# A linear-attention and softplus-MLP kernel: raw weights in two half tiles, four K buffers, and the second pass's attention a step earlier and ahead of softplus

## The chip, the cores and the metric

The kernel runs on one NeuronCore of a Trainium2 chip. The metric is the device time of one execution in microseconds. Before the change it was 609.94 us, the median of three runs (608.14 to 610.45).

## The reference

The reference is a delta-rule attention followed by a two-layer MLP on its output.

```python
B, H, S, D = 4, 8, 768, 48
k_n = k / (norm(k) + 1e-06)
state = zeros(B, H, D, D)
for t in range(S):
    y[:, :, t] = q_t @ state
    v_old = k_t @ state
    state = state + beta_t * outer(k_t, v_t - v_old)
x = y laid out as (B * S, H * D)          # 3072 x 384
h = x @ w_in                              # 384 x 2048
g = maximum(h, 0) + log1p(exp(-abs(h)))   # softplus
out = g @ w_out                           # 2048 x 384
```

## The kernel before

The sequence is cut into 12 chunks of 64 tokens (`NS`, `C`). A chunk of all 4 batches and 8 heads gives 256 rows of x, and each chunk has one MLP **pass** (0 to 11) over the 2048 hidden units, in 8 **steps** of two weight tiles of 128 units. Step (s, g) is step g of pass s.

One step puts out, in this order: the matmuls of `hidden(s, g)` with its three ScalarE functions (abs, exp, ln), a share of background work on DVE (`pull`, up to a budget in estimated ns), `softplus` of the step (one DVE instruction in pass 0, three after it, since g is then kept as a high and a low part), the attention blocks planned for the step, the conversion of weights (pass 0 alone), the splits of weights planned in `SPLITS`, and the output matmuls of the step before (`output(*late)`), which need that step's softplus. The order of the code is the order on each engine: the schedule is manual, and every engine works through its own list in order.

The attention of a chunk runs beside the MLP of the chunk before. It is a chain of blocks, placed by `at(s, g, cost, ...)`: `gram` (products of K with itself, for two chunks at a time), `invert` (the solution of 32 small triangular systems on DVE, in the background), `finish` (its two transposes), `cross_a` and `cross_b` (which join the half blocks), `arrange`, `masked_keys` (K against the state and Q, mask), `corrected` (the corrected values u), `result` (`y_all`, which makes x of that pass and moves parts of it by DMA, then `state` and the load of the next Q). `drain` runs the background to its end.

Weights come as 8-byte words of which two pieces make one f32: per tile one transfer into `ST[f]`, in the slot named `w{f+1}`. ScalarE copies the top piece (`top_half`, L402), DVE puts both together in place (`convert`, L410), and pass 0 multiplies with that f32 tile (`HF[f]`). From pass 1 on each f32 is used as a high part and a rest: `split(f)` casts on ScalarE into the first half of slot `w{f}` (L427) and subtracts on DVE into the second (L428). Slot `w{f}` held `HF[f-1]`, so tile f can be cast when tile f-1 has been subtracted. Three K buffers serve the chunks, with a fourth cut out of the slot behind the last weight tile from chunk 6 on. All DMAs are issued on SP, in order.

Of the kernel before, what the change touches and what calls it, by code (L numbers as in the profile page):

```python
# [40 lines left out]
def deltanet_moe(ctx, tc, kT, qT, kI, vN, beta, wts, out):  # L41
# [71 lines left out]

    n_tmp, spare = HB * HB // 4, []

    def last_slot():
        if not spare:
            assert len(W) == NF
            spare.append(one.tile([P, NP * C + 2 * n_tmp], F32, name=f"w{NF}"))
        return spare[0]  # L120

# [58 lines left out]
    def invert(u):  # L180
# [28 lines left out]
        if u < N16:  # L209

            parts = one.tile([P, 2, NP, HB + QB], F32, name=f"x{u + 1}")
            for j in range(2):
# [5 lines left out]
        if u < 2:
            tmp = (one, two)[u].tile([P, 2 * n_tmp], F32, name=("x0", "gl")[u])
        else:  # L220
            tmp = last_slot()[:, NP * C:]
# [165 lines left out]


    def load_weights(f):
        ST[f] = one.tile([P, 4 * DM], I32, name=f"w{f + 1}")  # L390
        if f >= AHEAD:
            nc.vector.tensor_copy(ST[f][:, 0:1], ST[f - AHEAD][:, 0:1])
        nc.sync.dma_start(ST[f].bitcast(U16)[:, 0:8 * DM - 1], wts[f][:, 1:8 * DM])

    def top_half(f):

        t, h = [a.bitcast(dt).rearrange("p (n w) -> p n w", w=w)  # L400
                for a, dt, w in ((tops[f % 2], F16, 2), (ST[f], BF16, 4))]
        nc.scalar.copy(t[:, :, 1], h[:, :, 2])  # L402

    def convert(n=1):
        for _ in range(n):
# [3 lines left out]
            words = ST[f].rearrange("p (n w) -> p n w", w=2)
            nc.vector.scalar_tensor_tensor(ST[f][:, 0:2 * DM], words[:, :, 0], 13, tops[f % 2],  # L410
                                           op0=ALU.logical_shift_right, op1=ALU.bitwise_or)
            HF[f] = ST[f][:, 0:2 * DM].bitcast(F32)
# [95 lines left out]
    with tc.manual_schedule(engines={ET.PE, ET.DVE, ET.Activation, ET.Pool, ET.SP}):  # L508
# [96 lines left out]

        def masked_keys(s, *gs):
            for g in gs:
                keys(s, g)
# [160 lines left out]
```

## Time and profile before

| | us |
|---|---|
| median of the runs | 609.94 |
| the profiled execution | 611.22 |
| its span (first to last instruction) | 609.5 |
| matmul engine (PE) busy | 569.4 (93%) |
| DVE busy | 447.4 (73%) |
| ScalarE (ACT) busy | 355.1 (58%) |
| GpSimd (POOL) busy | 31.2 (5%) |

The page of the profile gives for each group of instructions the busy time, the mean of one in ns, and the idle time of its engine ahead of it with what ended it. In the chain that ended last PE has 69%, DVE 17% and ACT 8%; the output matmuls (L474) have 28% and the hidden matmuls (L446) 27% of the span. Of the 40 slices of the span PE is busy at eight tenths or more in all but the first three, the tenth (seven) and the last; the granted clock is at seven tenths in the fifth slice and at eight in two around 137 to 168 us.

### The profile page before, as it was taken

Reading aid. Unit: us, or ns where it says so; the run is one execution under the profiler, and the core shown is the slowest. Engines: PE = TensorE matmul, PEld = TensorE weight load, DVE = VectorE, ACT = ScalarE, POOL = GpSimd, SP = SyncE. Lnnn points to the kernel's source line nnn. Section 1 sums busy time; section 2 is a strip of 40 time slices with the busy share of each in tenths; the row PEclk is TensorE's granted clock in tenths of the full one; section 3 lists DMA queues with packets and bytes.
Section 4 is the critical chain, followed back from the end, with each engine's and each line's share of the span. In section 5 each row is a group of like instructions: output and inputs, shape, how many; then the busy total and the mean of one; then the engine's idle time right before and its main releaser. Section 6 shows DMA issues by size and latency. Waiting matters only on the chain.

```text
span 609.5 us, 19848 instructions
## 1 busy us (share of the span) xinstructions
PE 569.4 (93%) x8630; PEld 531.0 (87%) x8630; DVE 447.4 (73%) x987; ACT 355.1 (58%) x703; POOL 31.2 (5%) x55
## 2 busy tenths in 40 slices
PE   5568899997889999999999999999999999999996
PEld 4447676797779999999999999999999999999996
DVE  5978679756677998989888989798888345354443
ACT  4344666776654767655766646775646485554443
POOL 5210000001000001000000000000000000000000
PEclk9999799998899999999999999999999999999999
DMA  9913851301042030132211141300120300300000
GB/s 201 320 55 104 247 205 53 68 29 27 27 89 84 9 61 29 54 67 80 43 26 54 36 91 49 67 29 9 48 66 28 66 30 2 66 29 14 27 0 27
DMA packets 33015, 39.81 MB, mean 65 GB/s; under 512 B 22432, under 2 KB 25600, under 8 KB 32928
## 3 DMA queue, kind: packets, MB, share of 16 engines
q1 hardware_dynamic: 32928, 38.54, 24.0%
q8 instruction: 68, 1.11, 0.8%
q14 instruction: 19, 0.16, 0.1%
HBM read 31.55 MB, written 4.72 MB: 60 GB/s over the span
## 4 chain that ended last, share of the span: by engine, by line
PE 69%; DVE 17%; ACT 8%; DMA 2%; issue 2%; SPq 1%; ACTq 0%; DVEq 0%
PE po L474 28%; PE ph L446 27%; PE pa L366 3%; PE pa L305 3%; DVE Z L233 2%; PE pa L351 2%; PE pa L339 2%; DVE w L410 2%; PE pa L131 2%; DVE w L228 2%; ACT w L427 1%; DVE big L317 1%; ACT a L451 1%; DVE a L457 1%; DVE w L428 1%
## 5 line engine op out<-in xcount | busy, mean ns | idle before, releaser
L446 PE MATMUL ph<-x,w 128*128 128x256 f32 x1680 | 229.5, 290 | 4.0 <-DMA x<-x 3.1
L446 PEld LDWEIGHTS ph<-x,w 128*128 128x128 f32 x1680 | 219.6, 191 | 10.4 <-issue 2.6
L474 PE MATMUL po<-w,gh 128*128 128x384 f32 x768 | 171.8, 364 | 3.9 <-DVE gh L459 3.9
L450 ACT ACTIVATE a<-ph 128x512 f32<-128x512 f32 x96 | 57.4, 598 | 169.4 <-PE ph L446 169.3
L474 PEld LDWEIGHTS po<-w,gh 128*128 128x128 f32 x768 | 133.3, 192 | 16.9 <-DVE gh L459 4.7
L457 DVE SCALAR_TENSOR_TENSOR a<-ph,a 128x512 f32<-128x512 f32 x88 | 60.4, 686 | 94.8 <-ACT a L452 94.7
L474 PE MATMUL po<-w,gl 128*128 128x384 f32 x352 | 78.4, 339 | 0.0
L474 PEld LDWEIGHTS po<-w,gl 128*128 128x128 f32 x352 | 63.8, 192 | 0.1
L460 DVE TENSOR_TENSOR gl<-a,gh 128x512 fp32r<-128x512 f32 x88 | 61.0, 693 | 3.0
L451 ACT ACTIVATE a<-a 128x512 f32<-128x512 f32 x96 | 60.7, 632 | 3.1
L452 ACT ACTIVATE a<-a 128x512 f32<-128x512 f32 x96 | 60.7, 632 | 3.1
L233 DVE TENSOR_TENSOR Z<-Z,w 128x30 f32<-128x30 f32 (+14 forms) x120 | 39.9, 332 | 4.1
L459 DVE CAST gh<-a 128x512 fp32r<-128x512 f32 x88 | 40.1, 456 | 3.0
L228 DVE TENSOR_TENSOR w<-Z,ltq 128x30 f32<-128x30 f32 (+14 forms) x120 | 39.6, 330 | 3.2
L317 DVE TENSOR_TENSOR big<-pa,maskP 64x256 f32<-64x256 f32 x88 | 37.0, 420 | 1.2
L366 PE MATMUL pa<-big 128*64 128x64 f32 x768 | 28.2, 232 | 1.1 <-ACT big L343 0.9
L366 PEld LDWEIGHTS pa<-big 128*64 128x64 f32 x768 | 25.7, 145 | 3.7 <-ACT big L343 1.8
L428 DVE TENSOR_TENSOR w<-w,w 128x768 fp32r<-128x768 f32 x16 | 15.3, 957 | 16.2 <-ACT w L427 16.1
L402 ACT CAST ex<-w 128x768 f16<-128x768 bf16 x16 | 16.8, 1060 | 17.7 <-DVE w L410 14.9
L285 POOL MEMSET tt<- 32x512 f32 x24 | 13.4, 558 | 265.6 <-ACT tt L283 262.2
L131 PE MATMUL pa<-kt 48*64 48x64 f32 x640 | 16.5, 261 | 11.1 <-DMA kt<-kT 10.9
L131 PEld LDWEIGHTS pa<-kt 48*64 48x64 f32 x640 | 14.7, 172 | 13.1 <-issue 7.6
(96 smaller groups left out, 538.9 us busy)
## 6 DMA issues: line engine op xcount, KB each, us to landing
w<-wts SPq DMA_DIRECT2D x16, 767.8 KB, 6.7
big<-qT SPq DMA_DIRECT2D x24, 192.0 KB, 4.2
nv<-vN SPq DMA_DIRECT2D x12, 384.0 KB, 3.4
ki<-kI SPq DMA_DIRECT2D x24, 192.0 KB, 4.6
out<-ex SPq DMA_DIRECT2D x24, 192.0 KB, 2.0
kt<-kT SPq DMA_DIRECT2D x20, 192.0 KB, 3.4
x<-x SPq DMA_DIRECT2D x66, 32.0 KB, 1.9
w<-kT SPq DMA_DIRECT2D x4, 192.0 KB, 4.3
```

The lines of the kernel that those rows point to most:

```text
L131: nc.tensor.matmul(pas[e][tk[t], i, :], k, k, start=True, stop=True)
L228: nc.vector.tensor_tensor(o, Z[:, a + j + 1:a + n, a + j:a + j + 1].to_broadcast([P, r, j]), lq[:, a + j:a + j + 1, a:a + j].to_broadcast( ...
L233: nc.vector.tensor_tensor(z, z, o, op=ALU.add)
L317: nc.vector.tensor_tensor(be[tk[ab], ab, e, 4 * g:4 * g + 4, 0:C], pks[e][t, :, 0:C], maskP[t].unsqueeze(1).to_broadcast([C, 4, C]), op=AL ...
L366: nc.tensor.matmul(py[tk[ab], i, :], big[:, at + C:at + 2 * C], big[:, at:at + C], start=True, stop=True)
L446: nc.tensor.matmul(ph[:, f], weight(s, 2 * g + f, a, k * P, P), xr[b][k], start=(c == 0), stop=(c == len(terms) * NK - 1))
L450: nc.scalar.activation(a, ph, AF.Abs)
L451: nc.scalar.activation(a, a, AF.Exp, scale=-1.0)
L452: nc.scalar.activation(a, a, AF.Ln, bias=1.0)
L457: nc.vector.scalar_tensor_tensor(a, ph, 0.0, a, op0=ALU.max, op1=ALU.add)
L460: nc.vector.tensor_tensor(hi_lo[1], a, hi_lo[0], op=ALU.subtract)
L474: nc.tensor.matmul(PO[s][:, h, 0:DM], hi_lo[b][:, f, h * P:(h + 1) * P], weight(s, 2 * g + f, a, DM, DM), start=(g == 0 and f == 0 and i = ...
```

## The change

It has four parts.

1. Raw weights come in two transfers per tile, into two half tiles: `RA[f]` in slot `a{f+1}` and `RB[f]` in slot `b{f}`. The copy of the top pieces and the conversion are each done in two halves; the converted tile lies in `RA[f]`. The high part goes into slot `b{f}`, where raw words lay that are no longer needed, the low part into slot `a{f}`, which held the converted tile f-1. Casts and subtractions have lists of their own, `HIGHS` and `LOWS`.
2. Four K buffers throughout; chunk 3's K is loaded near the start, chunk 4's where chunk 3's was. The scratch of the inversion has a tile of its own, and x has two buffers instead of three.
3. In pass 1 the attention blocks of chunk 2 stand one step earlier; the Gram matmuls of chunk 4 move from (0,7) to (0,4), those of chunk 5 from (1,5) to (0,7), where the next inversion also enters the background.
4. Softplus stands behind the blocks of its step instead of ahead of them, in every pass, and so behind the emptying of the background in the first step of odd passes, which pass 1 now has in this form too.

```diff
-STEP, EARLY, PULL0 = 3100, (4400, 3500, 3500), (500, 500, 3000)
-SPLITS = ((), (0,), (1,), (), (), (2,), (3,), (4,), (5,), (6, 7, 8), (9, 10), (11, 12), (13, 14), (15,), (), ())
+STEP, EARLY, PULL0 = 3100, (4100, 3500, 3500), (500, 500, 3000)
+HIGHS = {3: (0,), 4: (1,), 5: (2,), 6: (3, 4), 7: (5, 6), 8: (7, 8), 9: (9, 10), 10: (11,), 11: (12,), 12: (13, 14), 13: (15,)}
+LOWS = {6: (0,), 7: (1, 2, 3), 8: (4, 5, 6), 9: (7, 8, 9), 10: (10,), 11: (11,), 12: (12, 13), 13: (14, 15)}
...
-        kts[s] = KT[s if s < 2 else (1, 2, 3 if s > 2 else 2, 0)[s % 4]]
+        kts[s] = KT[s % 4]
...
+    tmp = const.tile([P, 2 * n_tmp], F32, name="tmp")
...
-        x = X[s] = one.tile([P, NK, n, B, C], ty, name=f"x{s % 3}")
+        x = X[s] = one.tile([P, NK, n, B, C], ty, name=f"x{s % 2}")
...
-        ST[f] = one.tile([P, 4 * DM], I32, name=f"w{f + 1}")
+        RA[f] = one.tile([P, 2 * DM], I32, name=f"a{f + 1}")
+        RB[f] = one.tile([P, 2 * DM], I32, name=f"b{f}")
         if f >= AHEAD:
-            nc.vector.tensor_copy(ST[f][:, 0:1], ST[f - AHEAD][:, 0:1])
-        nc.sync.dma_start(ST[f].bitcast(U16)[:, 0:8 * DM - 1], wts[f][:, 1:8 * DM])
+            nc.vector.tensor_copy(RA[f][:, 0:1], RA[f - AHEAD][:, 0:1])
+        for i, t in enumerate((RA[f], RB[f])):
+            nc.sync.dma_start(t.bitcast(U16)[:, 0:4 * DM - 1],
+                              wts[f][:, 4 * DM * i + 1:4 * DM * (i + 1)])
...
-    def split(f):
-
-        w = W[f] = one.tile([P, 2, 2 * DM], F32R, name=f"w{f}")
-        nc.scalar.copy(w[:, 0], HF[f])
-        nc.vector.tensor_tensor(w[:, 1], HF[f], w[:, 0], op=ALU.subtract)
+    def high(f):
+        assert f < done[0]
+        W[f, 0] = one.tile([P, 2 * DM], F32R, name=f"b{f}")
+        nc.scalar.copy(W[f, 0], HF[f])
+
+    def low(f):
+        W[f, 1] = one.tile([P, 2 * DM], F32R, name=f"a{f}")
+        nc.vector.tensor_tensor(W[f, 1], HF[f], W[f, 0], op=ALU.subtract)
...
         load_ki(0)
+        load_k(3)
         load_weights(1)
...
-        at(0, 7, 0, bind(load_beta, 2), bind(systems, 2), bind(gram, 4))
-        at(1, 0, 0, drain)
-        at(1, 1, 0, bind(cross_a, 2), bind(cross_a, 3))
-        at(1, 2, 920, bind(cross_b, 2), bind(cross_b, 3), bind(scale_v, 3), bind(arrange, 2))
-        at(1, 3, 2400, bind(masked_keys, 2, 0), bind(arrange, 3))
-        at(1, 4, 2400, bind(masked_keys, 2, 1))
-        at(1, 5, 0, bind(corrected, 2))
-        at(1, 6, 1700, bind(result, 2), bind(load_k, 6))
-        at(1, 5, 0, bind(gram, 5), bind(start, 2, invert), pos=1)
+        at(0, 4, 0, bind(load_beta, 2), bind(systems, 2), bind(gram, 4))
+        at(0, 7, 0, bind(gram, 5), bind(start, 2, invert))
+        at(1, 0, 0, bind(cross_a, 2), bind(cross_a, 3))
+        at(1, 1, 920, bind(cross_b, 2), bind(cross_b, 3), bind(scale_v, 3), bind(arrange, 2))
+        at(1, 2, 2400, bind(masked_keys, 2, 0))
+        at(1, 3, 2400, bind(masked_keys, 2, 1), bind(arrange, 3))
+        at(1, 4, 0, bind(corrected, 2))
+        at(1, 5, 1700, bind(result, 2))
...
-                softplus(s, g)
-                if s > 2 and s % 2 and g == 0:
+                if s % 2 and g == 0:
...
                 for block in blocks[0]:
                     block()
+                softplus(s, g)
...
-                for f in splits:
-                    split(f)
+                for f in highs:
+                    high(f)
+                for f in lows:
+                    low(f)
```

SP's list at the start, where the loads of K (kt), of weights (w), of V, Q and of K in its other layout (ki) are issued. Before:

```order
L100 DMA ki<-kI 64x768 x2
L393 DMA w_106<-wts 128x3071
L393 DMA w_219<-wts 128x3071
L88 DMA kt_74<-kT 48x1024 x2
L104 DMA nv<-vN 128x768
```

And now:

```order
L98 DMA ki<-kI 64x768 x2
L86 DMA kt_77<-kT 48x1024 x2
L386 DMA a_112<-wts 128x1535
L386 DMA b_113<-wts 128x1535
L386 DMA a_229<-wts 128x1535
L386 DMA b_230<-wts 128x1535
L102 DMA nv<-vN 128x768
```

The load of chunk 3's K has moved ahead of the second and the sixth weight tile, into a buffer of its own, and each weight tile has two transfers.

ScalarE's list in pass 1, from the functions of step (1,1) to those of step (1,3); casts of weights write w before, b now. Before:

```order
L450 ACTIVATE a<-ph 128x512
L451 ACTIVATE a<-a 128x512
L452 ACTIVATE a<-a 128x512
L277 ACTIVATE off<-pa 32x8x32 x8
L427 CAST w_1676<-w_603 128x768
L427 CAST w_1679<-w_691 128x768
L427 CAST w_1682<-w_799 128x768
L450 ACTIVATE a<-ph 128x512
L451 ACTIVATE a<-a 128x512
L452 ACTIVATE a<-a 128x512
```

And now:

```order
L452 ACTIVATE a<-a 128x512
L285 COPY tt<-pa 32x8x32 x8
L272 COPY tt<-tt 32x16x32 x2
L424 CAST b_1878<-a_941 128x768
L424 CAST b_1880<-a_1042 128x768
L450 ACTIVATE a<-ph 128x512
L451 ACTIVATE a<-a 128x512
L452 ACTIVATE a<-a 128x512
L424 CAST b_1953<-a_1049 128x768
L450 ACTIVATE a<-ph 128x512
```

Before, step (1,1) has the copies of cross_a and three casts; now it has those of cross_b, the copies of arrange and two casts, and step (1,2) has one.

DVE's list around step (3,5), which makes x of chunk 4 (x is the rest that is subtracted; the softplus of the step writes a, gh and gl). Before:

```order
L457 SCALAR_TENSOR_TENSOR a<-ph,a 128x512
L459 CAST gh<-a 128x512
L460 TENSOR_TENSOR gl<-a,gh 128x512
L374 TENSOR_TENSOR x_3470<-pa,x_3470 128x3x128
L376 TENSOR_TENSOR x_3471<-pa,x_3471 128x128
L374 TENSOR_TENSOR x_3470<-pa,x_3470 128x3x128
L376 TENSOR_TENSOR x_3471<-pa,x_3471 128x128
L228 TENSOR_TENSOR w_2217<-Z,ltq 128x108
```

And now:

```order
L222 TENSOR_TENSOR Z<-Z,tmp 128x4x27
L363 TENSOR_TENSOR x_3546<-pa,x_3546 128x3x128
L365 TENSOR_TENSOR x_3547<-pa,x_3547 128x128
L363 TENSOR_TENSOR x_3546<-pa,x_3546 128x3x128
L365 TENSOR_TENSOR x_3547<-pa,x_3547 128x128
L457 SCALAR_TENSOR_TENSOR a<-ph,a 128x512
L459 CAST gh<-a 128x512
L460 TENSOR_TENSOR gl<-a,gh 128x512
L217 TENSOR_TENSOR tmp<-Z,ltq 128x130
```

The four subtractions for x now stand ahead of the step's softplus, and the background (L217 and L222, before L228 and L233) follows.

## Rows read from the trace of the kernel before

**Rows 1.** Windows: passes 0, 1, 2, 4 and 5, from their first hidden matmul to the next pass's, and two microseconds in pass 1. Columns: length, then busy time of PE, PE's weight loads, DVE, ACT and POOL (with numbers of instructions), granted clock of PE as a share, share of the DMA engines, GB/s.

```profile
56.50:117.50 61.00, 56.39 (x731) 41.01 (x729) 48.00 (x103) 38.95 (x68) 1.03 (x2) 0.92 0.45 137
117.50:174.60 57.10, 50.47 (x815) 46.46 (x813) 34.12 (x54) 42.15 (x83) 3.45 (x5) 0.94 0.14 37
174.60:223.70 49.10, 46.17 (x625) 44.10 (x625) 42.65 (x109) 26.31 (x57) 0.00 (x0) 0.97 0.33 72
...
268.20:311.90 43.70, 43.70 (x626) 42.37 (x626) 38.69 (x83) 26.05 (x55) 0.00 (x0) 1.00 0.23 56
311.90:355.80 43.90, 43.90 (x754) 42.62 (x753) 37.48 (x90) 29.05 (x61) 3.61 (x5) 1.00 0.18 44
...
147.00:149.00 2.00, 2.00 (x7) 2.00 (x7) 1.97 (x6) 0.35 (x1) 0.17 (x1) 0.50 0.00 0
```

**Rows 2.** Timeline of PE in pass 1: start, length, operation, and in brackets the idle time before it and what ended it. L474 is output, L305 keys, L351 state.

```profile
131.70 1.66 PE L474 MATMUL po<-w,gh 128*128 128x384 f32 x8
...
136.12 1.00 PE L305 MATMUL pa<-big,kt 48*64 48x112 f32 x32
...
146.77 2.83 PE L474 MATMUL po<-w,gh 128*128 128x384 f32 x8 [2.29 <-DVE gh L459]
...
166.56 1.65 PE L351 MATMUL pa<-big,ki 128*48 128x48 f32 x64 [0.85 <-ACT off L144]
```

**Rows 3.** Waits in pass 1 (117.4 to 174.6): who waited for whom, us in total, times, longest.

```profile
DVE w L428 <- ACT w L427: 12.2, 9, 2.6
ACT w L427 <- DVE w L428: 10.8, 5, 4.4
```

**Rows 4.** The same view of pass 2 (174.6 to 223.7).

```profile
PE pa L305 <- DMA big<-qT: 1.5, 2, 1.1
...
PE ph L446 <- DMA x<-x: 1.4, 2, 0.7
```

**Rows 5.** Timeline of PE in the prelude. L131 is Gram (of chunk 3), L506 the warming matmuls, L252 and L259 the two products of the join.

```profile
24.67 2.59 PE L131 MATMUL pa<-kt 48*64 48x64 f32 x64 [6.63 <-DMA kt<-kT]
27.18 5.48 PE L506 MATMUL pa<-kt 48*128 48x512 f32 x6
32.60 1.90 PE L252 MATMUL pa<-tt,x 32*32 32x16 f32 x128
34.99 1.91 PE L259 MATMUL pa<-x,tt 32*32 32x16 f32 x128 [0.49 <-ACT x L254]
```

**Rows 6.** Timeline of DVE in the prelude: the second transpose of `finish`, the first of the next inversion, and the join's subtraction.

```profile
27.66 1.88 DVE L241 STREAM_TRANSPOSE tt<-Z 128x1024 f32<-128x1024 f32 x1
...
32.40 2.06 DVE L187 STREAM_TRANSPOSE ltq<-work 128x1024 f32<-128x1024 f32 x1
36.97 0.42 DVE L260 TENSOR_TENSOR tt<-tt,pa 128x256 f32<-128x256 f32 x1 [2.50 <-PE pa L259]
```

**Rows 7.** The page's part on DMA issues: number, size of each, median us from issue to landing.

```profile
w<-wts SPq DMA_DIRECT2D x16, 767.8 KB, 6.7
```

**Rows 8.** Groups of instructions on ACT, different shapes apart: busy us, mean ns of one, idle us before them with what ended it.

```profile
L452 ACT ACTIVATE a<-a 128x512 f32<-128x512 f32 x96 | 60.7, 632 | 3.1
...
L277 ACT ACTIVATE off<-pa 32x256 f32<-32x256 f32 x46 | 17.2, 374 | 2.5 <-DVE off L275 1.3 <-PE pa L269 0.4
L402 ACT CAST ex<-w 128x768 f16<-128x768 bf16 x16 | 16.8, 1060 | 17.7 <-DVE w L410 14.9 <-issue 2.8
...
L427 ACT CAST w<-w 128x768 fp32r<-128x768 f32 x16 | 13.3, 830 | 10.9 <-DVE w L428 10.8
```

**Rows 9.** The same view of DVE from 100 to 480 us.

```profile
L317 DVE TENSOR_TENSOR big<-pa,maskP 64x256 f32<-64x256 f32 x64 | 26.9, 420 | 0.9
L428 DVE TENSOR_TENSOR w<-w,w 128x768 fp32r<-128x768 f32 x14 | 13.4, 957 | 13.0 <-ACT w L427 12.9
...
L309 DVE TENSOR_TENSOR nv<-nv,pa 128x192 f32<-128x192 f32 x32 | 9.8, 347 | 0.0
...
L201 DVE TENSOR_TENSOR ltq<-ltq,ncT 128x1024 f32<-128x1024 f32 x4 | 4.9, 1223 | 0.0
```

**Rows 10.** The chain that ended last: start, length, operation. Pieces in a row give the time one kind of matmul group takes on PE: Gram (L131), hidden (L446), cross_a (L269), output (L474) of step (0,7) in f32 and of later passes.

```profile
120.13 2.58 PE po L474 x8
...
286.75 1.09 PE pa L131 x64
...
312.03 2.15 PE ph L446 x18
314.17 1.24 PE pa L269 x83
315.42 2.28 PE po L474 x12
```

**Rows 11.** Timeline of DVE in pass 5: the norms of step (5,0), the last subtraction for x in step (5,5), first and last instruction of softplus of step (5,6).

```profile
316.55 0.35 DVE L163 RECIPROCAL r<-rt 128x32 f32<-128x32 f32 x1 [1.85 <-ACT rt L161]
...
346.98 0.28 DVE L376 TENSOR_TENSOR x<-pa,x 128x128 fp32r<-128x128 f32 x1
...
351.62 0.69 DVE L457 SCALAR_TENSOR_TENSOR a<-ph,a 128x512 f32<-128x512 f32 x1 [1.03 <-ACT a L452]
...
352.81 0.69 DVE L460 TENSOR_TENSOR gl<-a,gh 128x512 fp32r<-128x512 f32 x1
```

**Rows 12.** Timeline of PE in pass 5: the output matmuls that need that softplus.

```profile
353.69 1.55 PE L474 MATMUL po<-w,gh 128*128 128x384 f32 x8
```

More of the change, by code (lines that the diff above doesn't have):

```diff
@@ L65, in deltanet_moe @@
              for ab in range(2)]
-    KT = [const.tile([P, NP, C], F32, name=f"kt{i}") for i in range(3)]
+    KT = [const.tile([P, NP, C], F32, name=f"kt{i}") for i in range(4)]
     big = const.tile([P, 2 * NP * QW + 16], F32, name="big")
@@ L76, in deltanet_moe @@
     half = const.tile([P, 1], F32, name="half")
-    W, HF, ST, OFF, TT, LTD, LDS, NN, NV, X, PK, bet, kts = ({} for _ in range(13))
+    W, HF, RA, RB, OFF, TT, LTD, LDS, NN, NV, X, PK, bet, kts = ({} for _ in range(14))
     tops = [two.tile([P, 2 * DM], I32, name="ex") for _ in range(2)]
@@ L82, in load_k @@
     def load_k(s):
-        if s == 6:
-            KT.append(last_slot()[:, 0:NP * C].rearrange("p (a c) -> p a c", c=C))
-        kts[s] = KT[s if s < 2 else (1, 2, 3 if s > 2 else 2, 0)[s % 4]]
+        kts[s] = KT[s % 4]
         for ab in range(2):
@@ L111, in parity @@
         return t.rearrange("p (a e) c -> p e a c", e=2)
[L114 to L120, printed above, removed]
+    n_tmp = HB * HB // 4
+    tmp = const.tile([P, 2 * n_tmp], F32, name="tmp")
     def systems(u):
@@ L217, in invert @@
                                      AF.Copy, scale=half)
[L218 to L221, printed above, removed]
         nc.vector.tensor_copy(Z.rearrange("p a b -> p (a b)")[:, 0:HB * HB:HB + 1], cT)
@@ L389, in load_weights @@
     def load_weights(f):
-        ST[f] = one.tile([P, 4 * DM], I32, name=f"w{f + 1}")
+        RA[f] = one.tile([P, 2 * DM], I32, name=f"a{f + 1}")
+        RB[f] = one.tile([P, 2 * DM], I32, name=f"b{f}")
         if f >= AHEAD:
-            nc.vector.tensor_copy(ST[f][:, 0:1], ST[f - AHEAD][:, 0:1])
-        nc.sync.dma_start(ST[f].bitcast(U16)[:, 0:8 * DM - 1], wts[f][:, 1:8 * DM])
+            nc.vector.tensor_copy(RA[f][:, 0:1], RA[f - AHEAD][:, 0:1])
+        for i, t in enumerate((RA[f], RB[f])):
+            nc.sync.dma_start(t.bitcast(U16)[:, 0:4 * DM - 1],
+                              wts[f][:, 4 * DM * i + 1:4 * DM * (i + 1)])
     def top_half(f):
-        t, h = [a.bitcast(dt).rearrange("p (n w) -> p n w", w=w)
-                for a, dt, w in ((tops[f % 2], F16, 2), (ST[f], BF16, 4))]
-        nc.scalar.copy(t[:, :, 1], h[:, :, 2])
+        t = tops[f % 2].bitcast(F16).rearrange("p (i n w) -> p i n w", i=2, w=2)
+        for i, raw in enumerate((RA[f], RB[f])):
+            h = raw.bitcast(BF16).rearrange("p (n w) -> p n w", w=4)
+            nc.scalar.copy(t[:, i, :, 1], h[:, :, 2])
     def convert(n=1):
@@ L408, in convert @@
                 return
[L409 to L412, printed above, removed]
+            for i, raw in enumerate((RA[f], RB[f])):
+                words = raw.rearrange("p (n w) -> p n w", w=2)
+                h = slice(i * DM, (i + 1) * DM)
+                nc.vector.scalar_tensor_tensor(RA[f][:, h], words[:, :, 0], 13, tops[f % 2][:, h],
+                                               op0=ALU.logical_shift_right, op1=ALU.bitwise_or)
+            HF[f] = RA[f].bitcast(F32)
             done[0] = f + 1
@@ L434, in weight @@
     def weight(s, f, a, c, n):
-        return W[f][:, a, c:c + n] if s else HF[f][:, c:c + n]
+        return W[f, a][:, c:c + n] if s else HF[f][:, c:c + n]
     def hidden(s, g):
@@ L554, in deltanet_moe @@
         pts = [p_half(0, g, ps_h, "ph") for g in range(2)]
-        load_k(3)
         load_v(1)
@@ L558, in deltanet_moe @@
             load_weights(f)
+        load_k(4)
         run(iv)
@@ L611, in masked_keys @@
             if 1 in gs:
-                for i in (s + 3,) * (s < 3) + (s + 4,) * (2 < s < NS - 4):
-                    load_k(i)
+                if s + 4 < NS:
+                    load_k(s + 4)
         def corrected(s):
@@ L691, in deltanet_moe @@
                 cost, *blocks = plan.pop((s, g), (0, (), ()))
-                splits = SPLITS[8 * s + g] if s < 2 else ()
+                highs, lows = [x.get(8 * s + g, ()) for x in (HIGHS, LOWS)]
                 if s == 0:
@@ L695, in deltanet_moe @@
                 hidden(s, g)
-                room = min(room, 0) + (STEP if s > 2 else EARLY[s]) - cost - 960 * len(splits)
+                room = min(room, 0) + (STEP if s > 2 else EARLY[s]) - cost - 960 * len(lows)
                 room = pull(room)
-                softplus(s, g)
-                if s > 2 and s % 2 and g == 0:
+                if s % 2 and g == 0:
                     for w in background[:] if s + 3 > NS - 1 else background[:-1]:
```

## The prediction

> **What bounds the kernel now.** I read the windows by pass first, then the matmul engine's timeline of the two passes that are long, then what the other engines wait for there.
>
> The windows [rows 1] cut the span at the first hidden matmul of a pass. Passes 4 and 5 (the fifth and sixth) have the matmul engine busy for all of 43.7 and 43.9 us at a granted clock of 1.00: there the kernel is bound by its matmuls, and nothing that leaves them alone can make these passes shorter. Pass 0 is nearly so (56.39 busy of 61.00). Pass 1 takes 57.1 us for work that pass 5 does in 43.9, and pass 2 takes 49.1 for work that pass 4 does in 43.7. So some 13 and 5 us are there to be had, and a few more in the prelude.
>
> [...] In pass 2 the start waits for transfers: 1.4 us for x and 1.5 us for q [rows 4], since y of pass 2 was ready late in pass 1.
>
> **The change part by part.** Zero of a sum is the profiled execution, 611.22 us (span 609.5 and 1.7 around it); the median of the runs shown is 609.94, 1.28 lower, and I subtract that at the end.
>
> (a) K of chunk 3 is loaded into a buffer of its own, ahead of the second weight tile instead of behind p_half. Before, the Gram matmuls of chunk 3 waited 6.63 us for it, started at 24.67 and pushed the warming matmuls (5.48) and so the join (from 32.60) back, although the join's other input was there when L241 ended at 29.54 [rows 5, 6]. It needs to land only some 3 us sooner for the join to start at 29.54, and it now passes two weight tiles, which take 6.7 us each to land [rows 7]. The join then runs 29.54 + 1.90 + 0.49 + 1.91 = 33.8, and DVE, free when L187 ends at 34.46, begins L260 there instead of at 36.97: 2.5 us, its whole idle time [rows 5, 6]. From both sides: 2.5 at most, nothing if the transfer lands no sooner. Against it stand the halves: the cast of a tile's top words (1060 ns for 768 words [rows 8]) becomes two of 384, and so does the conversion on DVE. An instruction of 512 words takes 632 ns on ScalarE [rows 8], so two halves cost between 1.06 and 1.26; I take 0.1 to 0.15 more per tile, and on the prelude's chain three such places: 0.4. Elsewhere in pass 0 they lie beside the matmuls. [...] No row here has the half alone. Term: **-2.1**.
>
> (b) The Gram of chunk 5 moves from pass 1 into step (0,7): 64 matmuls, 1.1 us [rows 10], on the engine that bounds pass 0. I take the rest of pass 0 as unchanged: softplus moves behind the blocks, but DVE there has less to do (the casts of tiles 0 and 1 and their subtractions leave steps 1 and 2). Term: **+1.1**.
>
> (c) Pass 1. High parts now go where dead raw words lay, so ScalarE can cast ahead and waits for no subtraction; the 10.8 and 12.2 us go. What is late next? I set zero at the end of hidden (1,0) and add along each engine, with the prices of [rows 2, 8 to 11]. Matmuls up to output (1,2): cross_a 1.24, output (0,7) 2.6, hidden 2.15, cross_b 1.24, output 2.28, hidden 2.15, keys 1.0, output 2.28, hidden 2.15, keys 1.0: 18.1. ScalarE starts 0.5 late (two casts of step (0,7) lie in front), then the functions 1.9, eight copies of cross_a 3.15, two casts 1.7, two copies out of 384 words 0.9 (between those of 256 and of 512), functions 1.9, eight copies 3.0, two copies of 512 words 1.3, two casts 1.7, functions of (1,2) 1.9: 18.0. DVE has the subtraction of tile 9 in front of the keys; its cast ends at 15.2, so the subtraction at 16.1, the keys (2 x 0.35 and 4 x 0.42, with gaps 2.3) at 18.4 and softplus (351.62 to 353.50 in pass 5) at 20.3. Output (1,2) is thus 2.2 us late. After it, ScalarE has caught up. At (1,6) the norms of the next system stand before softplus: functions 1.9, two small activations 0.5, four small DVE operations 1.05, softplus 1.85, together 5.3, against output 2.28 and hidden 2.15: 0.9 late. With a matmul-bound pass of 43.9 (row of pass 5), 0.3 for the slower f32 output of (0,7), 3.1 of lateness, and one stretch of low clock as behind the 2.29 us (2.83 - 1.66 = 1.2), that is 48.5 instead of 57.1. From both sides: 44.2 if nothing is late, 53 if the queue on ScalarE is as long as its present waits. Term: **-8.6**.
>
> (d) Pass 2. Result of chunk 2 stands at (1,5) instead of (1,6), one step of about 5 us before x and q are needed; the 1.4 and 1.5 us [rows 4] go, and the low clock behind them. DVE's inversion brings two small latenesses, 0.4 at (2,0) and 0.5 at (2,6), worked as at (1,6). 43.7 + 0.9 = 44.6 for 49.1; bounds 43.7 and 47. Term: **-4.5**.
>
> (e) Given back later. Softplus now stands behind the blocks in every pass. Where keys stand first, DVE uses the time in which it waited for ScalarE, and the output comes a keys step later: hidden. It is not hidden behind y. In pass 5 the x parts on DVE ended at 347.26; softplus of (5,5) can now start only there and ends at 349.1 (needed by 349.3, an output of 2.28 and a hidden of 2.15 before 353.69), and the eight background operations, which ended at 350.59 (1.03 before 351.62), run to 352.5. Softplus of (5,6) ends at 354.4, where the output matmuls started at 353.69 [rows 10 to 12]. I take 0.6 for the step with y in passes 3, 5 and 7: 1.8. At (5,0) softplus waited for the norms (DVE idle 1.85 [rows 11]), and L201 (1.2 [rows 9]) is now drawn in front of it: 0.7 late. At (6,6) four operations are drawn in front, as at (1,6): 1.0. At (3,0) the scaling and a transpose are drawn in front: 0.4 more than now. Passes 8 to 11 have no inversion and lose nothing. Bounds 0 and 8. Term: **+3.9**.
>
> Splitting the weight transfers adds 16 issues on SP; the tiles are converted several steps after they land, and I cost it at nothing. New tmp and x slots remove waits that no row shows. Sum: -2.1 + 1.1 - 8.6 - 4.5 + 3.9 = -10.2; 611.2 - 10.2 = 601.0, and against the median **599.7 us**.
>
> **Rivals.** *Nothing is given back* (DVE drains its queue in the steps without blocks, so (e) is 0): 595.8. For it: DVE is busy in only 37.5 of 43.9 us of pass 5 [rows 1]. Chance 0.20.
> *ScalarE's queue of pass 1 stays long*: the lateness at (1,2) is repeated at (1,3) and (1,4), each with low clock, some 2 x (1.3 + 1.2) = 5 us: 604.7. For it: ScalarE was busy 42.15 of 57.1 us [rows 1], which in 48.5 us is 87%. Chance 0.17.
> *The waits only change their name*, (c) and (d) are nothing: 609.94 - 2.1 + 1.1 + 3.9 = 612.8. Against it: the casts waited for a slot, not for work. Chance 0.06.
> *Softplus comes too late everywhere*: in passes 3 to 7 some 25 steps have blocks, each now in front of softplus by 1.7 to 2.3 us of DVE work; if the output matmuls wait 0.6 at each (15 us) and six of these bring low clock (7), (e) is 22 and the time 618, slower than before. It decides once the waits add to 14 us. For it: softplus ended only 0.19 us before its matmuls at (5,6) [rows 11, 12]. Against it: a wait of 0.85 us was not followed by low clock, one of 2.29 was [rows 2]. [...] Chance 0.06.
>
> **How the numbers follow.** The forecast has 0.51, with 596 to 603. About 0.5% (3 us) is what a measurement can tell from no change: 606.9 to 613.0. Faster: 0.51 + 0.20 + 0.16 of the queue's 0.17 = 0.87; same: 0.06 + 0.01; slower 0.06. The range reaches over the first two rivals to 594 and 606.5.
>
> **What would show it.** Right: in the profile after, pass 1 takes 47 to 50 us and pass 2 44 to 46; DVE and ScalarE no longer wait for one another in the splits; DVE's wait before L260 of the prelude (now L249) is gone; small waits for gh appear at the steps behind y in passes 3, 5 and 7. Wrong: pass 1 over 53 us, or the matmul engine under 95% busy in passes 4 to 7, which would mean that moving softplus costs more than the earlier attention gives.

## The result and the profile after

The changed kernel took 591.0 us (median of 4 runs, 588.42 to 592.98) against 610.01 for the kernel before: a ratio of 0.969, 95% interval 0.964 to 0.974. A second set of runs gave 589.67 (5 runs, 588.88 to 592.85; ratio 0.968, 0.9655 to 0.9706). Faster was forecast, but by 10, and the time lies below the range of 594.0 to 606.5. The profiled execution took 592.98 (span 591.3), 18.2 less than that of before.

The windows of the changed kernel, cut like [rows 1] at the first hidden matmul of a pass; passes 0, 1, 2, 4 and 5:

```profile
54.20:114.70 60.50, 55.83 (x793) 40.84 (x793) 45.95 (x111) 43.13 (x87) 1.04 (x2) 0.92 0.51 145
114.70:161.40 46.70, 45.21 (x750) 42.34 (x749) 39.67 (x68) 38.69 (x75) 3.35 (x5) 1.00 0.22 54
161.40:205.30 43.90, 43.72 (x625) 42.31 (x625) 41.35 (x104) 25.95 (x54) 0.00 (x0) 1.00 0.20 52
249.30:293.00 43.70, 43.70 (x626) 42.37 (x625) 38.63 (x83) 26.05 (x55) 0.00 (x0) 1.00 0.23 56
293.00:337.00 44.00, 43.92 (x754) 42.60 (x753) 37.07 (x91) 29.04 (x61) 3.35 (x5) 1.00 0.16 43
```

Pass 1 fell from 57.1 to 46.7 us, pass 2 from 49.1 to 43.9, and neither has low clock any more. Passes 4 and 5 are where they were. By the forecast's terms (from the starts of the first hidden matmuls, profiled execution against profiled execution):

| term | forecast | measured |
|---|---|---|
| (a) start of pass 0 | -2.1 | -2.25 (56.47 to 54.22) |
| (b) pass 0 | +1.1 | -0.5 |
| (c) pass 1 | -8.6 | -10.4 |
| (d) pass 2 | -4.5 | -5.2 |
| (e) passes 3 to 7 | +3.9 | +0.2 (219.64 to 219.85) |
| passes 8 to 11 | 0 | 0.0 (166.1 in both) |
| sum | -10.2 | -18.2 |

The largest gap is (e): nothing was given back. In pass 1 the waits of [rows 3] have shrunk to one line, and the cast on ScalarE has none for the subtraction:

```profile
DVE a L428 <- ACT b L424: 1.3, 1, 1.3
```

What PE still waits for behind pass 0 is mostly this (timeline of PE; steps (1,2), (1,6), (2,0) and (6,6)), and 1.12 us at the last output, where the kernel before waits as long:

```profile
136.15 0.44 PE L474 MATMUL po<-b,gh 128*128 128x384 f32 x1 [0.35 <-DVE gh L459]
...
159.22 0.44 PE L474 MATMUL po<-b,gh 128*128 128x384 f32 x1 [0.93 <-DVE gh L459]
...
170.18 0.41 PE L474 MATMUL po<-b,gh 128*128 128x384 f32 x1 [0.18 <-DVE gh L459]
...
379.06 0.44 PE L474 MATMUL po<-b,gh 128*128 128x384 f32 x1 [0.28 <-DVE gh L459]
```

The releaser is L459, the cast that makes gh, and not L460, the subtraction that makes gl and ends softplus. That is the key to (e), as DVE's and PE's timelines at step (5,6), the place of [rows 11, 12], show. DVE:

```profile
333.44 0.68 DVE L457 SCALAR_TENSOR_TENSOR a<-ph,a 128x512 f32<-128x512 f32 x1
334.16 0.43 DVE L459 CAST gh<-a 128x512 fp32r<-128x512 f32 x1
334.62 0.69 DVE L460 TENSOR_TENSOR gl<-a,gh 128x512 fp32r<-128x512 f32 x1
```

and PE:

```profile
334.84 0.28 PE L446 MATMUL ph<-x,a 128*128 128x256 f32 x1
334.96 0.34 PE L474 MATMUL po<-b,gh 128*128 128x384 f32 x1
```

The output matmuls start at 334.96, behind the hidden ones and without a wait: 0.35 us before softplus ends (334.62 + 0.69 = 335.31), and 0.37 after gh is there (334.59). Only the last four of the twelve output matmuls read gl (in the last step of a pass the last two of each six).

### The profile page after: what moved, and what is told of

Same layout as the page of the kernel before. It is cut to its first block, busy times and chain, and to the rows that moved or that the text cites. A ratio compares the mean times of both kernels' runs of the same rounds, so it can differ in the third digit from the quotient of the medians.

```text
span 591.3 us, 19891 instructions
## 1 busy us (share of the span) xinstructions
PE 559.9 (95%) x8630; PEld 523.3 (88%) x8630; DVE 447.9 (76%) x1003; ACT 356.0 (60%) x719; POOL 30.2 (5%) x55
## 4 chain that ended last, share of the span: by engine, by line
PE 80%; DVE 10%; ACT 5%; issue 2%; DMA 1%; SPq 1%; ACTq 0%; DVEq 0%
PE po L474 33%; PE ph L446 32%; PE pa L355 3%; PE pa L294 3%; PE pa L328 2%; PE pa L340 2%; PE pa L124 2%; DVE ltq L180 1%; PE pa L258 1%; PE pa L281 1%; DVE a L457 1%; DMA kt<-kT 1%; DVE Z L222 1%; DVE tmp L217 1%; DVE ltq L194 1%
## 5 line engine op out<-in xcount | busy, mean ns | idle before, releaser
L446 PE MATMUL ph<-x,b 128*128 128x256 f32 x1056 | 193.3, 282 | 0.0
L446 PE MATMUL ph<-x,a 128*128 128x256 f32 x624 | 172.9, 300 | 1.8 <-DMA x<-x 1.6
L446 PEld LDWEIGHTS ph<-x,b 128*128 128x128 f32 x1056 | 168.1, 190 | 0.5
L474 PE MATMUL po<-a,gh 128*128 128x384 f32 x416 | 143.4, 367 | 0.0
L474 PE MATMUL po<-b,gh 128*128 128x384 f32 x352 | 124.4, 354 | 3.2 <-DVE gh L459 2.9
L446 PEld LDWEIGHTS ph<-x,a 128*128 128x128 f32 x624 | 119.7, 192 | 6.9 <-DMA x<-x 1.8
L457 DVE SCALAR_TENSOR_TENSOR a<-ph,a 128x512 f32<-128x512 f32 x88 | 60.5, 687 | 59.0 <-ACT a L452 58.4
L474 PEld LDWEIGHTS po<-a,gh 128*128 128x128 f32 x416 | 78.9, 191 | 8.0 <-issue 1.8
L474 PE MATMUL po<-b,gl 128*128 128x384 f32 x352 | 77.0, 334 | 0.0
L474 PEld LDWEIGHTS po<-b,gh 128*128 128x128 f32 x352 | 66.1, 188 | 9.0 <-DVE gh L459 3.6
L460 DVE TENSOR_TENSOR gl<-a,gh 128x512 fp32r<-128x512 f32 x88 | 61.0, 693 | 3.0
L451 ACT ACTIVATE a<-a 128x512 f32<-128x512 f32 x96 | 60.7, 632 | 3.1
L452 ACT ACTIVATE a<-a 128x512 f32<-128x512 f32 x96 | 60.7, 632 | 3.1
L474 PEld LDWEIGHTS po<-b,gl 128*128 128x128 f32 x352 | 62.3, 188 | 0.1
L222 DVE TENSOR_TENSOR Z<-Z,tmp 128x84 f32<-128x84 f32 (+14 forms) x178 | 54.3, 311 | 5.2
L217 DVE TENSOR_TENSOR tmp<-Z,ltq 128x84 f32<-128x84 f32 (+14 forms) x178 | 53.9, 309 | 3.6
L459 DVE CAST gh<-a 128x512 fp32r<-128x512 f32 x88 | 37.6, 427 | 3.0
```

The costliest lines, as they stand in the source:

```text
L217: nc.vector.tensor_tensor(o, Z[:, a + j + 1:a + n, a + j:a + j + 1].to_broadcast([P, r, j]), lq[:, a + j:a + j + 1, a:a + j].to_broadcast( ...
L222: nc.vector.tensor_tensor(z, z, o, op=ALU.add)
L446: nc.tensor.matmul(ph[:, f], weight(s, 2 * g + f, a, k * P, P), xr[b][k], start=(c == 0), stop=(c == len(terms) * NK - 1))
L451: nc.scalar.activation(a, a, AF.Exp, scale=-1.0)
L452: nc.scalar.activation(a, a, AF.Ln, bias=1.0)
L457: nc.vector.scalar_tensor_tensor(a, ph, 0.0, a, op0=ALU.max, op1=ALU.add)
```

## The experiments

Starts and lengths in us of one profiled execution each; "low clock" is the time at a granted clock of 0.5 in pass 0, which alone moves that pass by some 4.6 us (60.5 with 10.2 of it in the changed kernel, 55.9 with none in gl_first) and is looked at in the last section. A profiled execution can lie some us off the median for it, so the readings below go by passes, and each is of one execution.

| kernel | start of pass 0 | pass 0 | low clock | pass 1 | pass 2 | 3 to 7 | 8 to 11 | median of runs |
|---|---|---|---|---|---|---|---|---|
| before | 56.5 | 61.0 | 10.2 | 57.1 | 49.1 | 219.6 | 166.1 | 610.01 |
| changed | 54.2 | 60.5 | 10.2 | 46.7 | 43.9 | 219.9 | 166.1 | 591.0 |
| after_again | 54.6 | 58.0 | 3.4 | 46.7 | 43.9 | 219.9 | 166.1 | 589.67 |
| sp_ahead | 54.5 | 59.7 | 6.8 | 47.0 | 43.7 | 220.1 | 166.1 | 592.75 |
| gl_first | 54.7 | 55.9 | 0 | 48.2 | 43.9 | 223.4 | 168.2 | 598.69 |
| sp_ahead_gl_first | 55.5 | 60.7 | 10.2 | 47.7 | 43.7 | 221.8 | 168.0 | 598.76 |
| splits_old | 54.6 | 57.2 | 0 | 47.8 | 43.9 | 219.8 | 166.1 | 595.53 |
| slots_old | 54.6 | 58.2 | 3.4 | 55.3 | 44.1 | 219.7 | 166.1 | 599.29 |
| attn_late | 54.6 | 54.9 | 0 | 46.0 | 47.0 | 220.0 | 166.1 | 593.14 |
| slots_only | 56.4 | 58.5 | 0 | 50.8 | 46.6 | 219.7 | 166.1 | 599.59 |
| k3_late | 56.7 | 60.5 | 10.2 | 46.7 | 43.9 | 219.8 | 166.1 | 593.96 |

**Was the order of softplus free, or paid for elsewhere?** sp_ahead moves one line:

```
+                softplus(s, g)
                 if s % 2 and g == 0:
...
                     block()
-                softplus(s, g)
```

> Softplus back ahead of the attention blocks, all else as in the changed kernel. Theory A (the order costs nothing in passes 3 to 7, because DVE has the time there, and pays in pass 1, where the mask of the keys no longer stands behind a late softplus): passes 3 to 7 together 219.7 to 220 us as in both kernels, pass 1 longer than 46.7 by 2 to 4, in all 594 to 597 against the 593.0 of the profiled run of the changed kernel. Theory B (the forecast's: behind the blocks costs 3.9 in passes 3 to 7, hidden by something else in the changed kernel): passes 3 to 7 get 3 to 4 us shorter, some 589 to 590.

Passes 3 to 7 took 220.1 us, pass 1 47.0. So the order costs nothing in passes 3 to 7, as theory A says, but it also earns almost nothing in pass 1 (0.3 instead of 2 to 4): there theory A fell. This part of the change is worth nothing that can be told from these passes, either way.

**Why was the lateness of (e) not seen?** gl_first turns the order of the output matmuls round, so that they start when softplus has ended, as the forecast had counted (the start and stop flags move with the order):

```
-        terms.sort(key=lambda t: (t[1] if last else 0, t[2] == 2))
+        terms.sort(key=lambda t: (t[1] if last else 0, t[2] != 2))
```

> The output matmuls of a step take the four that need gl first instead of last; nothing else moves. Theory A (the forecast counted to the end of softplus, but the matmuls start on gh, 0.69 us earlier, so the lateness in passes 3 to 7 was hidden by those 0.69): the steps whose matmuls now start before softplus ends wait by that much: 0.58, 0.51, 0.33, 0.58, 0.36, 0.67, 0.32, 0.31 and 0.56 in passes 3 to 7, together 4.2 us there, and some 3 in passes 1 and 2; in all about 600. Theory B (DVE clears its queue in steps without blocks, so nothing was late): passes 3 to 7 longer by less than 1 us, in all about 594.

Passes 3 to 7 became 3.5 us longer, near theory A's 4.2. The waits that came (timeline of PE in passes 3 to 7 of gl_first) stand at steps (3,0), (3,6), (5,0), (5,6), (6,6) and (7,6):

```profile
212.41 0.76 PE L474 MATMUL po<-b,gl 128*128 128x384 f32 x3 [0.54 <-DVE ss L147]
...
245.63 0.62 PE L474 MATMUL po<-b,gl 128*128 128x384 f32 x2 [0.41 <-DVE gl L460]
...
301.51 0.76 PE L474 MATMUL po<-b,gl 128*128 128x384 f32 x3 [0.81 <-DVE gl L460]
...
334.57 0.62 PE L474 MATMUL po<-b,gl 128*128 128x384 f32 x2 [0.25 <-DVE gl L460]
...
379.50 0.79 PE L474 MATMUL po<-b,gl 128*128 128x384 f32 x3 [1.01 <-DVE gl L460]
...
423.89 0.45 PE L474 MATMUL po<-b,gl 128*128 128x384 f32 x1 [0.21 <-DVE gl L460]
```

These are the six steps that term (e) had named, at 0.4, 0.6, 0.7, 0.6, 1.0 and 0.6: together 3.2 against 3.9. The forecast had the right places and nearly the right sizes, for a kernel whose matmuls wait for gl. Elsewhere the expectation was off: passes 1 and 2 grew by 1.5 us together instead of some 3, and passes 8 to 11, for which it named nothing, by 2.1. There the one wait is at the last output, 1.84 instead of 1.12, and low clock follows it (timeline, then a window behind it):

```profile
586.69 0.62 PE L474 MATMUL po<-b,gl 128*128 128x384 f32 x2 [1.84 <-DVE gl L460]
```

```profile
588.00:590.00 2.00, 2.00 (x8) 1.79 (x6) 0.00 (x0) 0.00 (x0) 0.00 (x0) 0.50 0.00 0
```

sp_ahead_gl_first has both edits:

> Softplus ahead of the blocks and the output matmuls that need gl first, both together. Theory A (the order of softplus does make gl late behind y, which only the matmuls' order hides): of the waits that gl_first showed in passes 3 to 7, those at the steps behind y (0.41, 0.25 and 0.21) are gone, those for the background operations drawn in front of softplus at (3,0), (5,0) and (6,6) stay; passes 3 to 7 together 222 to 222.5 us, between 220.1 and 223.4. Theory B (the order of softplus makes nothing late): 223.4 as in gl_first.

Passes 3 to 7 took 221.8 us, 0.2 under the expected span, and the waits (same view) are those of the background work alone, at (3,0), (5,0) and (6,6):

```profile
217.35 0.94 PE L474 MATMUL po<-b,gl 128*128 128x384 f32 x4 [0.58 <-DVE ss L147]
...
305.76 0.58 PE L474 MATMUL po<-b,gl 128*128 128x384 f32 x2 [0.80 <-DVE gl L460]
...
383.24 0.44 PE L474 MATMUL po<-b,gl 128*128 128x384 f32 x1 [1.01 <-DVE gl L460]
```

So softplus behind y does make gl late at (3,6), (5,6) and (7,6); the matmuls that run on gh cover it. Of the 3.5 us that gl_first adds in passes 3 to 7, 1.6 (223.4 to 221.8) hang on the order of softplus, the other 1.9 come with either order. The rival "nothing is given back" had the right outcome by a wrong reason: DVE did not clear its queue in time.

**What shortened pass 1?** splits_old puts the casts and subtractions back into the old steps and keeps the new slots; slots_old also lets the high part go where tile f-1 lies:

```
+SPLITS = ((), (0,), (1,), (), (), (2,), (3,), (4,), (5,), (6, 7, 8), (9, 10), (11, 12), (13, 14), (15,), (), ())
+HIGHS = LOWS = dict(enumerate(SPLITS))
...
-        W[f, 0] = one.tile([P, 2 * DM], F32R, name=f"b{f}")
+        W[f, 0] = one.tile([P, 2 * DM], F32R, name=f"a{f}")
...
-        W[f, 1] = one.tile([P, 2 * DM], F32R, name=f"a{f}")
+        W[f, 1] = one.tile([P, 2 * DM], F32R, name=f"b{f}")
```

(in place of the tables HIGHS and LOWS of the change; the last four lines in slots_old only).

> Casts and subtractions of the weight splits at the steps where the kernel before had them (table SPLITS for both), the new slots kept. Theory A (the slots did it): ScalarE and DVE still don't wait for one another, pass 1 within 2 us of 46.7, in all 593 to 595. Theory B (the places did it, casts two steps ahead of the subtractions): pass 1 of 51 to 55 us, in all 598 or more.

> As splits_old, and the high part of tile f goes into the slot of the converted tile f-1 again (the names of the two half slots swapped), so each cast waits for the subtraction of the tile before it. Theory A (the slots did it): waits of cast for subtraction of some 10 us come back, pass 1 of 51 to 55 us, 4 or more us above splits_old. Theory B (the places did it): the same as splits_old within 1 us. Theory C (neither; the attention that was moved up by a place brought the gain): both within 2 us of the changed kernel.

Pass 1 took 47.8 and 55.3 us: the two names are worth 7.5, the steps 1.1 in pass 1 and 1.3 in pass 0 (57.2 against the 55.9 of gl_first, both without low clock). The medians differ by 3.8 only: the profiled execution of splits_old took 591.18 and had no low clock, its other three runs 595.50 to 596.54, of which there is no trace; all runs of slots_old took longer (597.76 to 600.66). In the waits of pass 1 of slots_old the pair of [rows 3] is back:

```profile
DVE b L428 <- ACT a L424: 11.3, 9, 3.1
ACT a L424 <- DVE b L428: 8.4, 5, 3.3
```

Of the 19.7 us most lie beside other work; at the end of the chain stand two waits on PE (timeline of slots_old), and behind each the granted clock is 0.50:

```profile
137.15 0.44 PE L474 MATMUL po<-a,gh 128*128 128x384 f32 x1 [3.18 <-DVE gh L459]
...
164.83 0.44 PE L474 MATMUL po<-a,gh 128*128 128x384 f32 x1 [2.52 <-DVE gh L459]
```

```profile
139.00:141.00 2.00, 2.00 (x9) 2.00 (x8) 1.42 (x4) 1.94 (x4) 0.00 (x0) 0.50 0.00 0
166.00:168.00 2.00, 2.00 (x8) 2.00 (x7) 1.91 (x5) 0.00 (x0) 0.00 (x0) 0.50 0.10 23
```

**And pass 2?** attn_late puts the attention of chunks 2 and 3 back by a place (two of its lines are shown), the Gram of chunk 5 back into pass 1 and that of chunk 4 back to (0,7):

```
-        at(1, 4, 0, bind(corrected, 2))
-        at(1, 5, 1700, bind(result, 2))
+        at(1, 5, 0, bind(corrected, 2))
+        at(1, 6, 1700, bind(result, 2))
```

> The attention of chunks 2 and 3 back in the steps of the kernel before (one place later in pass 1), all else as in the changed kernel. Theory A (the forecast's term d: y of chunk 2 one step later comes too late for x and q): waits for transfers of 2 to 3 us at the start of pass 2, pass 2 of 46 to 49 us instead of 43.9. Theory B (y was late before only because pass 1 itself was late, and without the waits between cast and subtraction a step of 5 us is enough): pass 2 within 1 us of 43.9, and the whole within 2 us of the changed kernel at the same clock.

Theory A holds: pass 2 took 47.0 us. Its keys waited for q (waits of pass 2 of attn_late, then a window behind it), and low clock followed:

```profile
PE pa L294 <- DMA big<-qT: 1.2, 1, 1.2
```

```profile
161.00:163.00 2.00, 2.00 (x8) 1.92 (x7) 2.00 (x5) 0.00 (x0) 0.00 (x0) 0.53 0.03 8
```

The higher place thus brings 3.1 in pass 2 and costs 0.7 in pass 1 and the Gram's 1.0 in pass 0 (55.9 against 54.9 without it). slots_only has the new slots and K buffers and nothing else of the change:

> The kernel before with the weights in half tiles, the new slots and four K buffers alone: the order of softplus, the places of attention, the places of the splits and the load of K of chunk 3 are those of before. Theory A (the slots bring nearly all of the gain of passes 1 and 2): pass 1 of 47 to 50 us and pass 2 of 44 to 46, in all 595 to 599. Theory B (the parts are needed together): pass 1 above 52 or pass 2 above 47, in all 601 or more.

50.8 and 46.6 us lie between the theories' numbers, and the 599.59 just above A's span: the slots alone bring 6.3 of the 10.4 in pass 1 and 2.5 of the 5.2 in pass 2. What is left there is 0.9 for gh and 1.4 for the corrected keys in pass 1, with low clock behind the latter (0.50 from 150 to 152), and 1.2 for q in pass 2. The order of softplus and the load of K change little in these passes (sp_ahead, k3_late), so the rest falls to the places of attention and of the splits. In pass 2 it is the attention (attn_late). In pass 1 the rest is 4.1 us, but either part put back alone costs 1.1 at most there (splits_old, attn_late), so it seems that one of them is nearly enough; no run adds one alone to slots_only.

**The prelude.** k3_late only moves the load:

```
-        load_k(3)
         load_weights(1)
...
+        load_k(3)
         load_v(1)
```

> K of chunk 3 loaded behind the first keys matmuls again, as before, all else as in the changed kernel. Theory A (the early load brought the prelude's gain): the first hidden matmul starts at 56 to 57 us instead of 54.2 to 54.7, and 2.3 us more in all. Theory B (the prelude gained by something else): it starts within 0.5 us of 54.5.

Pass 0 started at 56.7, 2.1 to 2.5 later than with the early load: theory A. DVE's wait before the join's subtraction, gone in the changed kernel, is back (timeline of DVE in k3_late):

```profile
37.05 0.42 DVE L249 TENSOR_TENSOR tt<-tt,pa 128x256 f32<-128x256 f32 x1 [2.22 <-PE pa L248]
```

**Can the clock of pass 0 be held?** after_again is the changed kernel; the others add idle products (each two matmul instructions) where PE waits. warm_01 has the last line only, warm_x the last two:

```
+        warm(2)
         gram(3)
...
         state(0)
+        warm(2)
...
-        at(0, 1, 0, bind(cross_a, 1), bind(arrange, 1))
+        at(0, 1, 0, bind(warm, 2), bind(cross_a, 1), bind(arrange, 1))
```

> The changed kernel with six idle matmuls of 512 columns more (about 0.9 us each, results unused), two in each of three stretches in which the matmul engine waits: before the Gram matmuls of chunk 3 (3.0 us), before the first hidden matmuls (1.6), and before the first join matmuls of step (0,1) (3.1). Theory A (the clock of pass 0 falls after these waits and stays up if they are filled): pass 0 takes 56 us in every run, all runs 587 to 590. Theory B (the clock falls at other places, or whatever is done there): runs still spread from 588 to 593, or all are 1 to 3 us longer because the filling itself is late.

> The changed kernel itself once more, on the same chip as the next two. Theory A (the clock of pass 0 falls or not by chance): runs from 588 to 593 again, and the ones without a stretch of low clock in pass 0 are some 4 us shorter. Passes 1 to 11 as in the first profile within 0.3 us each.

> The changed kernel with four matmul instructions of 512 columns more (two idle products, results unused) ahead of the first cross products of step (0,1), nowhere else. Theory A (the wait of 3 us there lets the clock fall, and filling it keeps it up; the other fillings only made the prelude late): first hidden matmul at 54.2 to 54.8, pass 0 of 55.5 to 57, median 588 to 589, below the changed kernel's by 1 to 3. Theory B (the clock falls by what is before it, the wait for x at the first hidden matmuls): the same spread and median as after_again within 1 us.

> The changed kernel with two idle products ahead of the first join matmuls in front of pass 0 and two at step (0,1), none ahead of the Gram matmuls of chunk 3. Theory A (the clock falls behind the wait for x, and the filling in front of it keeps it up): no low clock after 57 us, hidden (0,0) ends at 59.5 to 60.5, all runs 587.5 to 589.5, some 1 to 2 us below the changed kernel. Theory B (the filling only moves the start and the clock falls all the same): median of 590 to 592, as the changed kernel or slower.

Medians: warm_fill 590.03, after_again 589.67, warm_01 591.85, warm_x 590.68. In its profile warm_fill has a pass 0 of 55.7 us, but it starts that pass 2.5 later than after_again and still has low clock from 56.8 to 60.3; warm_01 starts at 54.9 and has it from 57 to 64, warm_x starts at 57.7 and has it from 60.0 to 63.4. So filling these waits doesn't keep the clock up, and theory A fell in all three. Nothing is gained in any of them, so no version here beats the changed kernel by what can be told apart. What decides whether the clock falls in pass 0 stays open; the other passes of after_again are those of the first trace within 0.1 us.

## Why the prediction was wrong, step by step

**(e), the step that failed (3.7 of the 8 us).** It said: "Softplus of (5,6) ends at 354.4, where the output matmuls started at 353.69", and took 0.6. The end of softplus is the end of gl; the matmuls start on gh, which is there 0.69 us of L460 earlier, so 354.4 - 0.69 = 353.7 is in time. All of (e) was counted that way. [rows 12] had it in its operands (gh), and the kernel's own sort key puts the terms with gl last. The runs showed 0.28 at (6,6) and nothing at the other five steps, and 3.2 when gl was needed first. The forecast's own six numbers, each less 0.69, leave 0.3 at (6,6) alone. With (e) alone put right the forecast is 596.0, still in the range; below it the time came by (c), (d) and (b) as well, 1.8, 0.7 and 1.6 us, and by 0.7 because the median of the changed kernel lies 2.0 under its profiled execution and not 1.28.

**(c), sizes.** The mechanism was right: casts and subtractions waited for one another over a slot [rows 3], and 7.5 of the 10.4 hang on the two slot names. At (1,2) 2.2 of lateness was forecast and 0.35 came: 0.69 is the same gl, and the rest my queues, where the masks of the keys on DVE, behind which softplus stands, ended 17.6 us behind hidden (1,0) instead of 18.4 and the matmuls were ready at 18.5 instead of 18.1. At (1,6) 0.9 was forecast and 0.93 came, by luck: I had counted 0.9 to the end of gl, for which gl_first waits 1.63 there, so two errors of 0.7 cancelled. I had missed that ScalarE waits there for DVE, which has a transpose in front of the norms (timeline of ACT in the changed kernel):

```profile
156.49 0.23 ACT L153 ACTIVATE rt<-rt 128x32 f32<-128x32 f32 x1 [0.46 <-DVE rt L152]
```

The low clock of 1.2 that I set for a lateness of 2.2, as it stands behind the 2.29 of the kernel before (0.50 from 147 to 149 [rows 1, 2]), didn't come. Against this PE was busy for 45.2 us, 1.3 more than in pass 5 (windows above), for which I had set 0.3; where the other 1.0 lies stays open.

**(d), sizes.** 0.9 of lateness in pass 2 was counted to the end of gl; 0.18 came. At (2,0) gl did end 0.76 behind the keys matmuls ahead of its own (170.76 against 170.00), but gh only 0.04; at (2,6), for which I had 0.5, gl itself was in time (203.28 against 203.39).

**(b), sign.** The Gram did cost 1.0 (attn_late), but "the rest of pass 0 as unchanged" was wrong: the splits' new steps alone give back 1.3 there (splits_old). The -0.5 compares like with like only by luck: both profiled executions had 10.2 us of low clock in pass 0.

**(a), right,** 2.25 for 2.1. Each half of a weight tile's cast took 0.62 us (626 and 621 ns in the groups below, changed kernel), so two take 0.19 more than the 1.06 of [rows 8], where I took 0.1 to 0.15:

```profile
L397 ACT CAST ex<-a 128x384 f16<-128x384 bf16 x16 | 10.0, 626 | 7.9 <-DVE a L407 7.8
L397 ACT CAST ex<-b 128x384 f16<-128x384 bf16 x16 | 9.9, 621 | 0.0
```

**The rivals.** That nothing is given back came true, but not by its reason. ScalarE's queue in pass 1 wasn't the bound (38.69 busy of 46.70): PE has no wait at (1,3) or (1,4). The waits did not only change their name: passes 1 and 2 lost 15.6 us. Softplus too late everywhere did not happen: in passes 3 to 7 the 0.28 at (6,6) is the only wait for it, and the granted clock there is 1.00 (205.30 to 425.20). No low clock follows the 0.93 of pass 1 either. The 7 us that this rival set for low clock behind six such waits no run shows.

Not every wait was followed by a fall of the clock: low clock came behind waits of 3.18 and 2.52 us (slots_old), 1.84 (gl_first) and 1.22 (attn_late), and not behind 0.93 (changed kernel, granted 1.00 from 159 to 161 and in all of pass 1), nor behind one of 1.65 in splits_old (granted 1.00 from 134 to 138), nor behind one of 2.94 at step (0,1) of after_again (timeline, then a window behind it):

```profile
68.66 0.27 PE L258 MATMUL pa<-tt,off 32*32 32x32 f32 x9 [2.94 <-issue]
```

```profile
70.00:72.00 2.00, 2.00 (x9) 1.29 (x8) 1.93 (x5) 1.91 (x5) 0.62 (x2) 1.00 0.59 232
```

So the length of a wait alone doesn't tell whether the clock falls behind it.

## What to carry to other kernels

Count lateness to the operand that the consumer reads first, not to the end of the function that makes all of them: an order of accumulation that puts the latest operand last hid 3.2 us here for nothing. And where two engines hand tiles to each other in turn, look at which dead buffer each result goes into: two names, with the same instructions in the same order, were worth 7.5 us of pass 1 in the profiled executions and 3.8 between the medians.

## What the hardware showed that I had not expected

The low clock of pass 0 comes and goes from run to run. The two traces of the changed kernel have 10.2 and 3.4 us of it. Of its nine runs (4 and 5) the five whose granted clock averaged 0.997 or more took 588.42 to 589.67 us, the four with 0.964 to 0.971 took 590.81 to 592.98. Most of that gap in the mean is a record in the prelude (0.50 for 30.7 us in both traces, 0.026 of the mean), which by the next paragraph says little. Without it, an estimate worked out from these two traces: the three longest runs (592.77 to 592.98) have 10.2 us of low clock in pass 0, two (589.67 and 590.81) have 3.4, and four (588.42 to 589.65) none. The same instructions of pass 0 took 60.5 us at a mean of 0.92 and, in gl_first, this:

```profile
54.70:110.60 55.90, 51.73 (x792) 38.63 (x793) 45.68 (x112) 43.58 (x87) 1.04 (x2) 1.00 0.54 156
```

Some 4.6 us of the changed kernel's time are thus outside what the change decides; for the kernel before there is one trace only, so there it isn't shown.

In the prelude the granted clock can't be taken from its record alone. For the six warming matmuls the record says 1.00 in the kernel before and 0.50 in the changed one (windows in that order),

```profile
29.20:31.20 2.00, 2.00 (x4) 0.85 (x3) 1.94 (x4) 1.89 (x4) 0.00 (x0) 1.00 0.20 61
```

```profile
24.00:26.00 2.00, 2.00 (x3) 0.72 (x3) 2.00 (x19) 1.82 (x5) 0.00 (x0) 0.50 1.04 394
```

and they took 5.48 us in both ([rows 5], and the changed kernel's 21.86 to 27.34). In warm_fill four of the same kind ran earlier in 1.98 us at a recorded 1.00, about half as long each:

```profile
16.54 1.98 PE L506 MATMUL pa<-kt 48*128 48x512 f32 x4
...
21.86 5.48 PE L506 MATMUL pa<-kt 48*128 48x512 f32 x6
```

By their length the kernel before ran these at the low clock too; the record of the fall seems to be missing there. The four timelines of them (k3_late and warm_fill are the other two) all have 5.48 us, and in the half-microsecond windows of the other ten traces the matmul engine is full for 5.0 us in a row with one or two matmuls in each; only six of the fourteen have low clock on record for them. In pass 0 record and length do agree: a hidden matmul of step (0,0) took 634 ns where the record says 0.50 and 379 elsewhere. The prelude's mean clock, and the mean of the span with it, says little when two runs are compared; the length of like instructions says more.

Step (0,1) has a wait of 3.06 us in the middle of one group of cross products, for which the profile names no releaser:

```profile
68.15 0.34 PE L258 MATMUL pa<-tt,off 32*32 32x32 f32 x9 [3.06 <-issue]
```

With idle products of 1.98 us ahead of the group it was 0.91 (warm_fill) or none (warm_01). That doesn't tell what it waits for, since the products only fill the time: the wait ends 2.7 to 3.7 us behind hidden (0,1) in each of the six traces with a timeline of it, warm_fill too (3.3). In the kernel before (2.11 us, to 70.76) and in the changed one a packet of 16 KB of the DMA queue for instructions (q8, 68 packets in the whole execution) starts 2.4 and 2.5 us before the wait ends, and the same holds of PE's three other waits without a releaser in the changed kernel (2.4 to 2.9 us). The changed kernel's packet (DMA view of 65.6 to 65.75 us), 2.5 us before 68.15:

```profile
q8 instruction: 1, 0.02, 46.4%
```

So PE may wait there for its own next instructions, beside DMA engines that the weights keep busy (share 0.95 from 65 to 68 us). No run tests this.
